# Spreading the modulation gradient's sums by pairs of bf16 products, and finishing the last section in two halves

## The chip, the cores and the metric

The kernel runs on one core of one Trainium2 chip. The metric is the device time of one execution in microseconds; several executions are timed and the median is given. Besides, one execution was recorded with the hardware profiler. PE is TensorE (PEld its weight loads), DVE VectorE, ACT ScalarE, POOL GpSimd, and SP SyncE, which here only issues DMAs. Each engine works through its own queue of instructions in order.

## The reference, cut to what matters

The reference is a block with two branches, forward, and its gradient with respect to all inputs for a given output gradient. x has 2048 rows of 576 columns.

```python
mod = (_silu(c) @ w_mod).reshape(c.shape[0], 6, 1, -1)
sa, ca, ga, sb, cb, gb = ...                      # six rows of 576
h = _layernorm(x) * (1 + ca) + sa
x = x + ga * _A_ref(h, A_w_r, A_w_i)              # 2-D FFT, filter, inverse FFT
h = _layernorm(x) * (1 + cb) + sb
x = x + gb * _B_ref(h, B_w_gate, B_w_up, B_w_down)  # (h Wg * h Wu) Wd
_out, _vjp = jax.vjp(_f, ...)
_grads = _vjp(grad_out)
```

The outputs are the block's result (out_0) and eight gradients. The change concerns the last two of them:

- out_8, the gradient of w_mod (576 x 3456). It falls into six sections of 576 columns, one for each of the six modulation rows. The gradient of a modulation row is a vector g of 576 numbers (a sum over all 2048 rows of x), and the section is the outer product of silu(c) and g.
- out_7, the gradient of c (576 numbers): for each row of w_mod the sum over all six sections of w_mod times g, and then times the derivative of silu.

For the sixth section, gb, the vector is the column sum of grad_out times the second branch's output.

## The kernel before, in words

Rows are dealt to 16 tiles of 128 partitions (row 16p + t lies in tile t). The stages follow one another: forward first branch, second branch's big products, the weight gradients, and then the tail, from line 731, in which the change lies. The tail has three transforms (t1, t2, t3: gradients back through the filter and the norms) and at last a loop over the 16 tiles (lines 1107 to 1149) that computes the second branch's output of each tile.

**The last loop.** Each tile t has two halves of 288 columns. For each half PE runs 36 matmuls (`u3p`, L1127) into a bank of PSUM, and ACT copies the bank to `ob` (L1128). DVE multiplies `ob` with the output gradient `got` to `pr` (L1134), then with the modulation row to `of` (L1136), and adds x1 (`x1t`) to `o0` (L1138), which a DMA on POOL's queue stores. `x1t` and `got` are loaded by POOL's queue for two tiles at a time, into one buffer each.

**Column sums.** A bank `csF` collects the sums of `pr` over all rows. `colsum` (L784) is a matmul with a table `pick` of ones that adds the first half of the columns on the bank's upper 64 rows and the second half on the lower 64. In the loop the sums of tile t - 2 are added after tile t's matmuls, and the last three tiles' after the loop's last matmuls. `add_zero` (L781) opens and closes the bank.

**Sections.** `section(j, halves, secp)` (L812) makes one sixth of out_8 and its share of out_7. Its vector first has to stand on all 128 partitions: `spread` (L803) multiplies it in float32 with a table (ones, `ones_f`, where the vector's parts are spread over rows, `of_rows`; a row selector, `sel`, where row 0 and row 64 hold the two halves, `of_sums`). Each of the two products leaves a bank with 288 columns; ACT copies the first to `dmb`, DVE the second (`evac`, L141 and L143). Then w_mod's section `wmj` is loaded by two DMAs on SP's queue (L817, L818); out_8's section `o8` is `dmb` scaled by silu(c), in five blocks of rows, shared by ACT (L832) and DVE or, in the last section, POOL (L834); two DMAs on SP's queue store it (L835, L836); and DVE multiplies `wmj` with `dmb` in five blocks, with a sum along the columns into `gsc` (L825). The buffers `dmb`, `wmj`, `o8` and `pr7` of the pool `secp` exist once.

Five sections are made within the loop, at tiles 9 to 13 (`late`, L1093, and L1129 to L1131). `tc.issue_after(mm.ins)` puts their PE instructions behind the tile's last matmul in PE's queue. The sixth, gb, follows the loop (L1150 to L1153): its sums are copied out of `csF` to `dgb`, spread, and finished with `last=True`, in which DVE's products come ahead of the scalings. Then (L1154 to L1168) `gsc` is summed, multiplied with the derivative (`gcf`), expanded to a 128 x 640 table (`gcd`) and turned into one row by two matmuls with ones, copied to `gcr` and stored as out_7.

**What sets the order.** The program lists instructions in the order of the Python text. A planner puts them into the engines' queues: it goes through a modelled time and gives each engine the instruction with the highest priority (the earliest in the program, where `tc.high_priority` does not change it) of those whose inputs it takes to be ready. It also adds the semaphores on which an instruction waits. On the chip a queue keeps this order whatever is late.

Of the kernel before, what the change touches and what calls it, by code (L numbers as in the profile page):

```python
# [19 lines left out]
NT = 16  # L20
S = 2048
D = 576
# [10 lines left out]
SPREAD = 40  # L33

# [50 lines left out]
def build(ctx, tc, A_x, A_w_r, A_w_i, B_w_gate, B_w_up, B_w_down, c_in, w_mod, grad_out,  # L85
# [39 lines left out]
    ones_f = glob.tile([128, 128], FP32, name="ones_f")  # L125
    nc.vector.memset(ones_f[:], 1.0)

# [603 lines left out]
    with ExitStack() as ts:  # L731
# [29 lines left out]
        sel = tl.tile([128, 2, 128], FP32, name="sel")  # L761
# [4 lines left out]
        gsc = tl.tile([128, 5, 6], FP32, name="gsc")  # L766
# [33 lines left out]
        def spread(lhs, src):  # L800

            pp = ps_fp.tile([128, 512], FP32, name="spp", tag="fp")
            nc.tensor.matmul(pp[:, 0:288], lhsT=lhs, rhs=src, start=True, stop=True)  # L803
            return pp[:, 0:288]

        def of_rows(d):
            return [lambda h=h: spread(ones_f[:], d[:, h * 288:(h + 1) * 288]) for h in range(2)]

        def of_sums(d):
            return [lambda h=h: spread(sel[:, h, :], d[:]) for h in range(2)]  # L810

        def section(j, halves, secp, last=False):  # L812
            dmb = secp.tile([128, D], FP32, name="dmb")
            for h in range(2):
                evac(dmb[:, h * 288:(h + 1) * 288], halves[h](), eng=("a" if h == 0 else "v"))
# [3 lines left out]
            o8 = secp.tile([128, 5, D], BF, name="o8")  # L819

            def products():
                for m in range(5):
                    r = RM[m]
                    pr7 = secp.tile([128, D], BF, name="pr7")
                    nc.vector.scalar_tensor_tensor(out=pr7[r, :], in0=wmj[r, m, :], scalar=1.0, in1=dmb[r, :], op0=MUL, op1=MUL, accum_out=gsc[r, m, j:j + 1])  # L825

            if last:
                products()
            for m in range(5):
                r = RM[m]  # L830
                if m % 2 == 0:
                    nc.scalar.activation(out=o8[r, m, :], in_=dmb[r, :], func=ACT.Copy, scale=sc_col[r, m:m + 1])  # L832
                else:
                    (nc.gpsimd if last else nc.vector).tensor_scalar(out=o8[r, m, :], in0=dmb[r, :], scalar1=sc_col[r, m:m + 1], scalar2=None, op0=MUL)  # L834
            nc.sync.dma_start(out_8[0:512, j * D:(j + 1) * D].rearrange("(m q) n -> q m n", q=128), o8[:, 0:4, :])  # L835
            nc.sync.dma_start(out_8[512:576, j * D:(j + 1) * D], o8[64:128, 4, :])  # L836
            if not last:
                products()
# [254 lines left out]
        late = {9: (MSB, of_sums(dsb)), 10: (MCB, of_rows(dcb)), 11: (MGA, of_rows(dga)), 12: (MSA, of_sums(dsa)), 13: (MCA, of_rows(dca))}  # L1093
# [12 lines left out]
        prs = {}  # L1106
        for tp_ in range(NT // 2):
# [13 lines left out]
            for ti in range(2):  # L1121
                t = 2 * tp_ + ti
                ob = o2p.tile([128, D], BF, name="ob3")
                for h in range(2):
                    p2 = ps_u3.tile([128, 512], FP32, name="u3p")
                    for fb in range(NFB):
                        mm = nc.tensor.matmul(p2[:, 0:288], lhsT=hls[fb // 9][:, fb % 9, ti * 128:(ti + 1) * 128], rhs=(wdA[:, fb] if fb < 15 else wdB[:, fb - 15])[:, h * 288:(h + 1) * 288], start=(fb == 0), stop=(fb == NFB - 1))  # L1127
                    nc.scalar.copy(ob[:, h * 288:(h + 1) * 288], p2[:, 0:288])  # L1128
# [3 lines left out]
                pr = prs[t] = o2p.tile([128, D], BF, name="pr3", bufs=3)  # L1132
                for h in range(2):
                    nc.vector.tensor_tensor(out=pr[:, h * 288:(h + 1) * 288], in0=ob[:, h * 288:(h + 1) * 288], in1=got[:, ti, h * 288:(h + 1) * 288], op=MUL)  # L1134
# [11 lines left out]
                for d_ in ([t - 2] if t < NT - 1 else [t - 2, t - 1, t]):  # L1146
# [80 lines left out]
```

## Time and profile before

| | us |
|---|---|
| median of three runs | 1588.66 (1585.04 to 1589.61) |
| profiled execution, its own time | 1585.66 |
| its span, first to last instruction | 1583.9 |
| granted TensorE clock, mean | 0.99 |
| PE busy, share of the span | 96% |
| DVE busy | 66% |
| ACT busy | 35% |
| POOL busy | 11% |
| last tile's last big matmul ends (u3p, L1127), from the span's start | 1569.7 |
| last instruction before the final store is issued (gcr, L1165) ends | 1580.9 |

Times within the execution count from the span's first instruction. A group of instructions is named by engine, line, output and inputs; "idle before" is the time for which the engine stood still ahead of it, and the arrow names what ended that. The chain of waits is followed back from the last instruction of the kernel.

### The profile page before, as it was taken

How to read it: one execution, taken by the hardware profiler on the slowest of the kernel's cores; microseconds unless marked ns; L12 is line 12 of the kernel's file. 1: busy time of each engine (PE TensorE's matmuls, PEld its weight loads, DVE VectorE, ACT ScalarE, POOL GpSimd, SP SyncE). 2: the span in 40 equal slices, each digit the busy share in tenths (PEclk: the TensorE clock that was granted, in tenths of full speed). 3: DMA queues.
4: the chain of work that ended last, by engine and by line, in shares of the span. 5: the costliest groups of instructions: out<-in, count | busy, mean ns of one | idle time of the engine just before them, and what ended most of it. 6: DMA issues, size and time to landing. Idle time of an engine off the chain costs nothing.

```text
span 1583.9 us, 29938 instructions
## 1 busy us (share of the span) xinstructions
PE 1526.4 (96%) x11300; PEld 1028.1 (65%) x11306; DVE 1043.3 (66%) x2626; ACT 559.4 (35%) x1120; POOL 172.3 (11%) x285
## 2 busy tenths in 40 slices
PE   6999999999999999999999999999999979799997
PEld 4665543566666666667666666766666666577775
DVE  6866663766666666666666666666666765678655
ACT  6667732322222222222222222222222356465022
POOL 0001221110010101001010100101000002000232
PEclk9999999999999999999999999999999999999999
DMA  9879997868685795877767786858976777547775
GB/s 323 268 197 235 289 261 211 172 133 158 123 177 114 159 153 118 168 132 155 141 148 136 143 163 122 173 116 144 139 141 137 193 207 200 212 144 214 278 228 156
DMA packets 485252, 280.33 MB, mean 177 GB/s; under 512 B 407634, under 2 KB 452435, under 8 KB 484211
## 3 DMA queue, kind: packets, MB, share of 16 engines
q1 hardware_dynamic: 459922, 185.50, 54.9%
q0 software_dynamic: 25184, 92.92, 19.7%
q8 instruction: 88, 1.44, 0.4%
q14 instruction: 58, 0.47, 0.1%
HBM read 108.48 MB, written 82.31 MB: 120 GB/s over the span
## 4 chain that ended last, share of the span: by engine, by line
PE 81%; DVE 6%; DMA 5%; issue 4%; ACT 3%; POOL 0%; SPq 0%; ACTq 0%; DVEq 0%; POOLq 0%
PE u57p L594 26%; PE u8p L676 18%; PE gup L647 16%; PE u4p L408 7%; PE u3p L1127 4%; PE gup L642 2%; DMA Xn<-xn_d 2%; DMA n2c<-n_d 2%; PE yp L186 1%; PE zp L908 1%; ACT u L1055 1%; PE zp L346 1%; DVE ln_st L151 1%; DMA xc<-in_A_x_dram 1%; DMA hh_sf<-hhT 1%
## 5 line engine op out<-in xcount | busy, mean ns | idle before, releaser
L681 DVE TENSOR_TENSOR acc<-acc,u8p 128x288 f32<-128x288 f32 x1088 | 489.2, 454 | 314.6 <-PE u8p L676 314.2
L676 PE MATMUL u8p<-wT,ggT 128*128 128x288 bf16 x1152 | 327.5, 286 | 1.7 <-DVE acc L681 1.7
L676 PE MATMUL u8p<-wT,guT 128*128 128x288 bf16 x1152 | 327.2, 286 | 0.0
L647 PE MATMUL gup<-h2T,wgu 128*128 128x512 bf16 x1152 | 294.9, 379 | 0.0
L597 ACT CAST so<-u57p 128x288 bf16<-128x288 f32 x216 | 86.0, 398 | 521.4 <-PE u57p L594 515.5
L594 PE MATMUL u57p<-gon,hh_sf 128*128 128x288 bf16 x1152 | 188.5, 286 | 0.5 <-DMA hh_sf<-hhT 0.5
L594 PE MATMUL u57p<-h2p,gg_sf 128*128 128x288 bf16 x1152 | 187.9, 286 | 0.0
L594 PE MATMUL u57p<-h2p,gu_sf 128*128 128x288 bf16 x1152 | 185.9, 286 | 0.0
L647 PEld LDWEIGHTS <-wgu 128*128 128x128 bf16 x1152 | 109.5, 98 | 98.8 <-issue 17.1
L676 PEld LDWEIGHTS <-ggT 128*128 128x128 bf16 x1152 | 112.6, 98 | 67.2 <-issue 14.0
L408 PE MATMUL u4p<-goT,wdT 128*128 128x512 bf16 x656 | 151.6, 380 | 0.6 <-DVE goT L380 0.5
L676 PEld LDWEIGHTS <-guT 128*128 128x128 bf16 x1152 | 112.7, 98 | 55.8 <-issue 2.2
L1127 PEld LDWEIGHTS <-hl 128*128 128x128 bf16 x1152 | 111.9, 99 | 32.9 <-issue 5.9
L594 PEld LDWEIGHTS <-hh_sf 128*128 128x128 bf16 x1152 | 112.7, 98 | 29.2 <-DMA hh_sf<-hhT 0.8
L594 PEld LDWEIGHTS <-gu_sf 128*128 128x128 bf16 x1152 | 112.5, 98 | 28.4
L594 PEld LDWEIGHTS <-gg_sf 128*128 128x128 bf16 x1152 | 112.5, 98 | 28.2
L649 ACT CAST gT<-gup 128x512 bf16<-128x512 f32 x144 | 84.3, 586 | 130.7 <-PE gup L647 130.7
L649 ACT CAST uT<-gup 128x512 bf16<-128x512 f32 x144 | 84.3, 585 | 73.5 <-PE gup L647 73.5
L408 PEld LDWEIGHTS <-wdT 128*128 128x128 bf16 x656 | 61.4, 98 | 73.1 <-issue 8.0
L1127 PE MATMUL u3p<-wdB,hl 128*128 128x288 bf16 x672 | 94.8, 290 | 5.3 <-DMA wdB<-in_B_w_down_dram 5.3
L660 POOL DMA_DIRECT2D hhT_d<-hhT x36 | 33.2, 921 | 504.4 <-DVE hhT L651 475.5
L141 ACT CAST ghh_st<-u4p 128x512 bf16<-128x512 f32 x88 | 51.2, 585 | 65.2 <-PE u4p L408 63.7
(357 smaller groups left out, 1701.7 us busy)
## 6 DMA issues: line engine op xcount, KB each, us to landing
ghhT_d<-ghh_st POOLq DMA_DIRECT2D x36, 512.0 KB, 4.4
ghh<-ghhT_d POOLq DMA_DIRECT2D x36, 512.0 KB, 7.3
hhT_d<-hhT POOLq DMA_DIRECT2D x36, 512.0 KB, 6.6
hl<-hhT_d SPq DMA_DIRECT2D x32, 576.0 KB, 7.2
out_dram<-woT SPq DMA_DIRECT2D x72, 128.0 KB, 2.0
wdn<-in_B_w_down_dram SPq DMA_DIRECT2D x18, 288.0 KB, 3.9
out_dram<-so SPq DMA_DIRECT2D x36, 144.0 KB, 2.6
wgu<-in_B_w_gate_dram SPq DMA_DIRECT2D x18, 256.0 KB, 3.4
```

The source lines that it names most:

```text
L141: nc.scalar.copy(dst, src)
L151: nc.vector.bn_stats(out=st[:, t, h, :], in_=xt[:, t, h * 288:(h + 1) * 288])
L408: nc.tensor.matmul(pt[:], lhsT=wdTs[k][:, j, m, :], rhs=goT[:, 4 * sb4:4 * sb4 + 4, m, :], start=(m == 0 and n == 5), stop=(m == n - 1))
L594: mm = nc.tensor.matmul(pw[0][:, 0:288], lhsT=sf[:, t, :], rhs=rhs_n[:, t, h * 288:(h + 1) * 288], start=(t == 0), stop=(t == NT - 1))
L597: nc.scalar.copy(so[:, h * 288:(h + 1) * 288], pw[0][:, 0:288])
L642: nc.tensor.matmul(pts[-1][:], lhsT=wgu[r, 8, jw * 128:(jw + 1) * 128], rhs=h2T[r, 4 * sb4:4 * sb4 + 4, 4, :], start=True, stop=False)
L647: nc.tensor.matmul(pts[k][:], lhsT=wgu[:, 4 * wi_ + m, jw * 128:(jw + 1) * 128], rhs=h2T[:, ts_, m, :], start=False, stop=(m == 3))
L649: nc.scalar.copy((gT, uT)[wi_][:, ts_, :], pts[k][:])
L660: nc.gpsimd.dma_start(hhT_d[:, :, fb, :].rearrange("tp f x -> f tp x"), hhT[:].rearrange("f (tp ti) p -> f tp (ti p)", ti=2))
L676: nc.tensor.matmul(pu[:, 0:288], lhsT=l_, rhs=r_, start=(k == 0), stop=(k == len(mms) - 1))
L681: nc.vector.tensor_tensor(out=dst, in0=dst, in1=pu[:, 0:288], op=ADD)
L1127: mm = nc.tensor.matmul(p2[:, 0:288], lhsT=hls[fb // 9][:, fb % 9, ti * 128:(ti + 1) * 128], rhs=(wdA[:, fb] if fb < 15 else wdB[:, fb - 1 ...
```

## The change

Four things change.

1. The vector is no longer spread by one float32 product. `two_parts` makes a bf16 copy (ACT) and the bf16 rest (DVE: the vector less the copy), and `spread` adds two bf16 products into the bank. `ones_f` goes, `sel` becomes bf16. The buffers of the two parts are of the pool `secp` and exist once for each of the two shapes (576 columns, `dr`, for cb, ga and ca; 288 columns, `ds`, for sb, sa and the sixth section's partial sum).
2. The sixth section's sums: `csF` collects tiles 0 to 10 only (`TURN`). At tile 12, after that tile's section, it is closed, and its two halves are spread by the row selector into two banks `csG`, on all 128 rows. The later tiles are added there by a product with ones (`ones_sum`), which leaves their sums on all rows too.
3. At the last tile, each half is finished by itself: DVE multiplies the bank of the big products with `got` directly, one matmul adds the sum to `csG`, and `last_half` scales and multiplies straight from that bank: five ACT instructions and five DVE products of 288 columns, and two stores on SP's queue. `wmj` of this section is loaded after the first half's matmuls. `dgb` and `dmb` are not used there, nor POOL. `gsc` has a seventh column for the second half.
4. The row of out_7 is made by five small matmuls with `gcf` itself as the stationary operand, one to a block of rows, in place of `gcd` and the two products; ACT copies 256 columns and DVE 320.

```diff
-    ones_f = glob.tile([128, 128], FP32, name="ones_f")
-    nc.vector.memset(ones_f[:], 1.0)
...
-        sel = tl.tile([128, 2, 128], FP32, name="sel")
+        sel = tl.tile([128, 2, 128], BF, name="sel")
...
-        gsc = tl.tile([128, 5, 6], FP32, name="gsc")
+        gsc = tl.tile([128, 5, 7], FP32, name="gsc")
...
+        def two_parts(pool, src, w, name):
+
+            hi = pool.tile([128, w], BF, name=name + "_hi")
+            lo = pool.tile([128, w], BF, name=name + "_lo")
+            nc.scalar.copy(hi[:], src)
+            nc.vector.tensor_tensor(out=lo[:], in0=src, in1=hi[:], op=SUB)
+            return hi, lo
+
+        def spread(out, lhs, parts, cols, stop=True):
+            for k, p_ in enumerate(parts):
+                nc.tensor.matmul(out, lhsT=lhs, rhs=p_[:, cols], start=(k == 0), stop=stop and k == 1)
+
+        def section_load(j, secp):
             wmj = secp.tile([128, 5, D], BF, name="wmj")
             nc.sync.dma_start(wmj[:, 0:4, :], w_mod[0:512, j * D:(j + 1) * D].rearrange("(m q) n -> q m n", q=128))
             nc.sync.dma_start(wmj[64:128, 4, :], w_mod[512:576, j * D:(j + 1) * D])
+            return wmj, secp.tile([128, 5, D], BF, name="o8")
+
+        def section_products(j, secp, wmj, sums, cols, slot):
+            for m in range(5):
+                r = RM[m]
+                pr7 = secp.tile([128, D], BF, name="pr7")
+                nc.vector.scalar_tensor_tensor(out=pr7[r, cols], in0=wmj[r, m, cols], scalar=1.0, in1=sums[r, :], op0=MUL, op1=MUL, accum_out=gsc[r, m, slot:slot + 1])
+
+        def section_store(j, o8, cols):
+            a0, a1 = j * D + cols.start, j * D + cols.stop
+            nc.sync.dma_start(out_8[0:512, a0:a1].rearrange("(m q) n -> q m n", q=128), o8[:, 0:4, cols])
+            nc.sync.dma_start(out_8[512:576, a0:a1], o8[64:128, 4, cols])
+
+        def section(j, d, secp):
+            rows = d.shape[1] == D
+            parts = two_parts(secp, d[:], d.shape[1], "dr" if rows else "ds")
+            dmb = secp.tile([128, D], FP32, name="dmb")
+            for h in range(2):
+                hs_ = slice(h * 288, (h + 1) * 288)
+                pp = ps_fp.tile([128, 512], FP32, name="spp", tag="fp")
+                spread(pp[:, 0:288], ones_b[:] if rows else sel[:, h, :], parts, hs_ if rows else slice(0, 288))
+                evac(dmb[:, hs_], pp[:, 0:288], eng=("a" if h == 0 else "v"))
+            wmj, o8 = section_load(j, secp)
...
+            section_store(j, o8, slice(0, D))
+            section_products(j, secp, wmj, dmb, slice(0, D), j)
+
+        def last_half(h, wmj, o8, secp, bank):
+            hs_ = slice(h * 288, (h + 1) * 288)
+            for m in range(5):
+                r = RM[m]
+                nc.scalar.activation(out=o8[r, m, hs_], in_=bank[r, 0:288], func=ACT.Copy, scale=sc_col[r, m:m + 1])
+            section_products(MGB, secp, wmj, bank[:, 0:288], hs_, 5 + h)
+            section_store(MGB, o8, hs_)
...
+        def ones_sum(t, h):
+            nc.tensor.matmul(csG[h][:, 0:288], lhsT=ones_b[:], rhs=prs[t][:, h * 288:(h + 1) * 288], start=False, stop=(t == NT - 1))
+
+        def sums(t):
+            for h in range(2):
+                if t > TURN:
+                    ones_sum(t, h)
+                else:
+                    colsum(csF, h, prs[t][:, h * 288:(h + 1) * 288])
+            if t == TURN:
+                add_zero(csF, first=False)
+                parts = two_parts(secp, csF[:, 0:288], 288, "ds")
+                for h, tag in enumerate(("csA", "csC")):
+                    csG.append(ps_cs.tile([128, 512], FP32, name="csG", tag=tag))
+                    spread(csG[h][:, 0:288], sel[:, h, :], parts, slice(0, 288), stop=False)
...
+                    if t == NT - 1:
+                        pr = pr_tile(t) if h == 0 else prs[t]
+                        nc.vector.tensor_tensor(out=pr[:, h * 288:(h + 1) * 288], in0=p2[:, 0:288], in1=got[:, ti, h * 288:(h + 1) * 288], op=MUL)
+                        if h == 0:
+                            last = section_load(MGB, secp)
+                            sums(t - 2)
+                            sums(t - 1)
+                        ones_sum(t, h)
+                        last_half(h, *last, secp, csG[h])
                     nc.scalar.copy(ob[:, h * 288:(h + 1) * 288], p2[:, 0:288])
...
-                for d_ in ([t - 2] if t < NT - 1 else [t - 2, t - 1, t]):
-                    for h in range(2):
-                        if d_ >= 0:
-                            colsum(csF, h, prs[d_][:, h * 288:(h + 1) * 288])
-        add_zero(csF, first=False)
-        dgb = tl.tile([128, 288], FP32, name="dgb")
-        nc.vector.tensor_copy(dgb[:], csF[:, 0:288])
-        section(MGB, of_sums(dgb), secp, last=True)
+                if 2 <= t < NT - 1:
+                    sums(t - 2)
...
-        gcd = secp.tile([128, 5, 128], BF, name="gcd")
-        nc.vector.tensor_tensor(out=gcd[:], in0=ident[:].unsqueeze(1).to_broadcast([128, 5, 128]), in1=gcf[:].unsqueeze(2).to_broadcast([128, 5, 128]), op=MUL)
         gcr = secp.tile([128, D], BF, name="gcr")
-        for m0, w in ((0, 4), (4, 1)):
+        for ms_, c0, w in (((0, 1), 0, 256), ((2, 3, 4), 256, 320)):
             pp = ps_fp.tile([128, 512], FP32, name="gcp", tag="fp")
-            nc.tensor.matmul(pp[:, 0:w * 128], lhsT=ones_b[:], rhs=gcd[:, m0:m0 + w, :].rearrange("p m n -> p (m n)"), start=True, stop=True)
+            for m in ms_:
+                r = RM[m]
+                nc.tensor.matmul(pp[0:1, m * 128 - c0:m * 128 - c0 + KD[m]], lhsT=gcf[r, m:m + 1], rhs=ident[r, 128 - KD[m]:128], start=True, stop=True)
...
```

47 lines of the change are left out of this document (14 added, 33 removed).

## The prediction

> **What bounds the kernel now.** I read the page's engine table first (PE is busy for 96% of the span), then the chain of waits in order of time, restricted to the last 85 us, then the timeline of each engine there, and last the tiles that the edits touch. The change acts only after 1450 us.
>
> The chain of waits, cut to the last stage; columns are start us, duration us, engine and line:
>
> ```profile
> 1510.48 0.97 PE spp L803 x4
> 1511.45 0.24 PE csF L784 x2
> 1511.69 8.82 PE u3p L1127 x72
> 1520.51 0.97 PE spp L803 x4
> ...
> 1560.90 8.83 PE u3p L1127 x72
> 1569.75 0.41 ACT ob L1128
> ...
> 1571.35 0.38 DVE dgb L1152
> 1571.73 0.04 issue
> 1571.78 1.25 PE spp L803 x4
> ```
>
> Until 1569.73 PE alone carries the chain: a tile of 72 matmuls takes 8.82 us (0.1225 each), and the spreading of a section stands between two tiles for 0.97 us. From there to the end, 14.2 us, the chain goes through single instructions. The timeline of the same stretch shows the costliest ones:
>
> ```profile
> 1573.60 2.23 ACT L832 ACTIVATE o<-dmb,sc_col 128x576 bf16<-128x576 f32 x3 [0.57 <-DVE dmb L143]
> 1573.60 0.76 DVE L825 SCALAR_TENSOR_TENSOR pr<-wmj,dmb 128x576 bf16<-128x576 bf16 x1
> 1573.68 4.29 POOL L834 TENSOR_SCALAR o<-dmb,sc_col 128x576 bf16<-128x576 f32 x2 [1.49 <-DVE dmb L143]
> 1574.40 1.18 DVE L825 SCALAR_TENSOR_TENSOR pr<-wmj,dmb 128x576 bf16<-128x576 bf16 x1
> ...
> 1578.86 0.83 DVE L1159 TENSOR_TENSOR gcd<-ident,gcf 128x640 bf16<-128x640 bf16 x1
> 1579.74 0.69 PE L1163 MATMUL gcp<-gcd,ones_b 128*128 128x512 bf16 x2 [6.72 <-DVE gcd L1159]
> 1580.36 0.57 ACT L1165 CAST gcr<-gcp 1x512 bf16<-1x512 f32 x1 [4.53 <-PE gcp L1163]
> 1580.96 0.32 SPq L1168 DMA_DIRECT2D out_dram<-gcr  x1
> ```
>
> DVE's five products go from 1573.60 to 1578.40, the two beside POOL's work taking 1.18 instead of 0.76. From the last copy's end (1580.93) to the span's end (1583.9) it is 2.95 us: the small store. Third, DVE's timeline at tile 10, where DVE is late:
>
> ```profile
> 1523.43 0.45 DVE L143 COPY dmb<-spp 128x288 f32<-128x288 f32 x1
> 1528.67 0.46 DVE L1138 TENSOR_TENSOR o<-of,x1t 128x576 bf16<-128x576 bf16 x1 [4.79 <-DMA x1t<-x_d]
> 1529.04 0.94 DVE L834 TENSOR_SCALAR o<-dmb,sc_col 128x576 bf16<-128x576 f32 x2
> 1530.25 0.76 DVE L825 SCALAR_TENSOR_TENSOR pr<-wmj,dmb 128x576 bf16<-128x576 bf16 x1 [0.26 <-DMA wmj<-in_w_mod_dram]
> ```
>
> DVE's products of tile 10's section start when PE is already at the end of tile 11 (1530.38). Those of the sections end at 1522.5, 1534.2, 1544.4, 1554.1 and 1562.3, paced by DMA (an x1t load, then wmj loads of 4 to 8 us), not by PE. PE does not notice, because nothing it needs from DVE is younger than two tiles.
>
> **The change part by part.**
>
> *Spreading in bf16.* Per section four float32 instructions (0.97 us) go and four bf16 matmuls of 288 columns (4 x 0.1225 = 0.49) come: 0.48 less on PE, five sections, **-2.4 us**.
>
> *What comes ahead of the last big matmul.* The sum of tiles 0 to 10 is spread early (four matmuls, 0.49, and a zero matmul of 512 columns, 0.22), the four column sums of tiles 13 and 14 move between the halves of tile 15 (0.49), and one sum of tile 15 with them (0.12): **+1.3 us**. The last big matmul ends 1.1 us earlier, at T = 1568.6.
>
> *High and low parts.* Each section now needs an ACT copy (128x576 from float32: 0.67 by the copy of the accumulator; 288: 0.40) and a DVE subtraction (float32 operands: 256 columns 0.42, 512 columns 0.68, so 576 about 0.75 and 288 about 0.45). ACT has 3.4 us of work per 10 us tile and DVE 5 to 8, so the busy time is hidden. The first two pairs can fall into the third transform's last steps at 1451 to 1457, where PE already waits 0.3 us at a time for ACT: 0 to 1.3 us, taken as 0, since the waiting ACT shows there is room. The order is the question: PE now waits for the subtraction, which stands in DVE's queue, in front of tensor products that wait for DMAs or behind them. For tile 11 the parts can be made only after tile 10's spreading has read the shared buffer (1520.9). In DVE's queue the subtraction then comes either before the instruction that waits for x1t (done at 1524: no wait), after the two scalings (1530.7), or after the products (1534.9). PE wants it at about 1529.4, with two savings behind it. So the wait is 0, 1.3 or 5.5 us. For the partial sum at tile 12 DVE can do it at about 1546 (products to 1544.4, then four instructions); PE arrives between 1541 and, if the planner put it late, after that: 0 to 5 us, and 7.5 if it stands behind the next products (1554.1). Those waits do not add fully, as DVE's clock is set by DMA: together 0 to 8 us. I take 0, by the row that shows the long DVE gap (4.79 us idle right where the subtraction is ready), and keep 8 for the range.
>
> *Tile 15, first half.* It ends 5.0 us before T (36 x 0.1225 plus the 0.6 moved in), 1563.6. DVE is free at 1563.8; product from the bank 0.45 (the accumulating addition of 288 columns out of a bank takes 0.454), sum matmul 0.38 with its hand-overs, five ACT scalings of 288 columns at 0.40 after the copy of the tile: 1564.7 to 1566.7. The wmj load starts at 1562.4, when the previous products free the buffer, and lands 3.7 to 5.0 us after its second part's issue at 1562.83: 1566.5 to 1567.8. Five products of 288 columns at 0.50 (0.80 from start to start at 576, less 288 columns at 1.02 ns): done 1569.3 to 1570.3. They precede the second half's product in the program, so that one starts 0.7 to 1.7 after T; I take **+1.2**. Queued behind it: the final sum and all that follows.
>
> *Tile 15, second half, and the finish.* Product 0.45; sum matmul 0.38; then five ACT scalings (2.0) and five DVE products (2.5) that read the same bank. In the trace of before every bank is read by one engine; no row shows two readers at once. If they run side by side the scalings cost nothing, one after the other 2.0 us. I take 2.0, since the nearest rows have a single reader. [...] Then the reduction 0.22, the product with the derivative 0.21, five small matmuls instead of the 0.83 expansion and two big ones (0.6 with latency, from the 0.28 of one matmul and four more behind it), the wider of the two copies (320 columns, 0.5), and the store 2.95. Sum: 0.45 + 0.38 + 2.0 + 2.55 + 0.22 + 0.21 + 0.6 + 0.5 + 2.95 = 9.9 us. The tile's own copy and output (0.40, 0.45, 0.45) fill DVE's wait for ACT; if that cover goes, 0.9 more. Both `dmb` copies, the float32 spreading (1.25), dgb, POOL's 4.29 and the slowed products go.
>
> *Queues.* SP issues four stores of the last section in place of two (0.85 us more), the first pair during the second half, the second pair at about T + 4.3, well ahead of the small store. POOL loses its two scalings. The removed ones table and the smaller selector stand in idle time: nothing.
>
> Sum: end at 1568.6 + 1.2 + 9.9 = 1579.7 against 1583.9, **-4.2 us**; on the profiled execution's own time 1581.5 (1585.66). That execution lies 3.0 us under the median of the runs shown; the four known executions average 1587.2, 1.6 above it, and I add these 1.6: **1583.1**, 0.35% under the median of 1588.66. I call 0.3% (4.8 us) about what a measurement of this kernel can tell from no change.
>
> **The rivals.**
>
> Side by side (0.19): ACT and DVE read the bank together. For: their data are ready at the same moment. Against: no row with two readers. -2.0: 1581.1.
>
> A short wait of PE (0.25): one subtraction stands after the scalings, or the partial sum's comes 2 to 4 us late. For: DVE's section work runs a tile behind PE. Against: DVE's idle 4.79 us. +3: 1586.1.
>
> A long wait (0.14), the one that ends slower: tile 11's subtraction stands behind tile 10's products in DVE's queue, because the planner believes wmj landed. PE stops 5.5 us at 1529, and again 2.5 at the partial sum: 8.0 in all, 1591.1. It decides from 5.6 us of waiting on. For: products are older in the program, and DVE did each section's five in one piece. Against: at 1523.9 wmj was 6 us from landing.
>
> The spreading saves nothing (0.05): if a pair of bf16 matmuls with its loads took the 0.97 again, 1585.5. Against: the colsum pairs take 0.24 on the chain.
>
> My own forecast has 0.37, with 1581 to 1585.5 as its own range.
>
> **How the numbers follow.** Faster by over 0.3% means under 1583.9: 0.6 of the forecast (0.22), nearly all of side by side (0.19), 0.06 of the others: 0.47. Slower by over 0.3%, above 1593.4: 0.04 of the long wait and 0.06 for an order changed elsewhere: 0.10. Same: 0.43. The range goes from side by side with the second half's 1.2 gone (1578.5) to the long wait (1591).
>
> **What would show it.** Right: in the chain, spreading of 0.49 between tiles and no PE wait for a subtraction; the last big matmul at 1568.6; scalings, then products, after it; 11 us to the end. Wrong: idle PE before a spreading, released by DVE; a last big matmul after 1571; scalings and products overlapping.

## The result, and the profile after

The changed kernel takes 1598.9 us (median of 7 executions, 1592.62 to 1609.42), against 1588.66 us for the kernel before (7 executions, 1585.04 to 1591.26). The ratio is 1.0078, with a 95% interval of 1.0057 to 1.01 (the two medians divided give 1.0064): the change makes the kernel slower by 0.8%, where I had forecast 1583.1 us, 0.35% faster. The profiled execution after took 1602.71 us, with a span of 1600.9 us.

The view to read first is again the chain of waits, here of the kernel after, from tile 10 on (start us, duration us, engine and line):

```profile
1530.46 8.38 DMA wmj<-in_w_mod_dram
...
1540.67 0.67 DVE dr_lo L803
...
1543.86 5.88 DMA wmj<-in_w_mod_dram
...
1554.78 6.78 DMA wmj<-in_w_mod_dram
...
1563.39 0.38 DVE ds_lo L803
1563.78 0.04 issue
1563.82 0.64 PE csG L808 x2
1564.46 6.97 PE u3p L1162 x47
1571.42 0.49 PE spp L808 x4
1571.91 0.24 PE csG L1127 x2
1572.16 8.82 PE u3p L1162 x72
```

In the kernel before, PE carried this stretch alone. Now, up to 1563.8, the chain runs through three loads of `wmj`, DVE's products that wait for them, and the subtraction that makes a low part; PE takes over only after that. The spreading of a section itself costs 0.49 us, as forecast. What PE waited for in the last stage (us in total, number of waits, longest):

```profile
PE csG L808 <- DVE ds_lo L803: 3.6, 1, 3.6
PE csG L808 <- ACT ds_hi L802: 3.2, 1, 3.2
PE spp L808 <- DVE dr_lo L803: 3.1, 1, 3.1
...
PE csG L1127 <- DVE pr L1165: 1.0, 1, 1.0
```

The first three are new: the low part of tile 11's section (3.1 us), and the high and the low part of the partial sum (3.2 and 3.6 us), 9.9 us together. DVE's and PE's timelines show the place of the last (start, duration, engine, line, output and inputs, and in brackets the idle time before it and what ended that):

```profile
1561.58 0.76 DVE L820 SCALAR_TENSOR_TENSOR pr<-wmj,dmb 128x576 bf16<-128x576 bf16 x1 [4.89 <-DMA wmj<-in_w_mod_dram]
...
1562.63 0.75 DVE L820 SCALAR_TENSOR_TENSOR pr<-wmj,dmb 128x576 bf16<-128x576 bf16 x1
...
1563.31 0.45 DVE L803 TENSOR_TENSOR ds_lo<-csF,ds_hi 128x288 bf16<-128x288 f32 x1
1563.68 0.75 DVE L820 SCALAR_TENSOR_TENSOR pr<-wmj,dmb 128x576 bf16<-128x576 bf16 x1
```
```profile
1563.82 0.64 PE L808 MATMUL csG<-ds_lo,sel 128*128 128x288 bf16 x2 [3.55 <-DVE ds_lo L803]
1564.25 2.76 PE L1162 MATMUL u3p<-wdB,hl 128*128 128x288 bf16 x11
```

ACT had made `ds_hi` by 1555.6, but the subtraction stands in DVE's queue behind the first two products of tile 12's section (and an addition between them), and the first product waits for its load. DVE does nothing for 4.89 us, with the subtraction ready, because the instruction at the head of its queue is not.

The wait of 3.2 us for the high part comes the same way by one more step, as ACT's timeline shows:

```profile
1554.87 0.40 ACT L139 COPY dmb<-spp 128x288 f32<-128x288 f32 x1 [3.44 <-DVE pr L820]
1555.16 0.41 ACT L802 CAST ds_hi<-csF 128x288 bf16<-128x288 f32 x1
```

The copy that makes `ds_hi` stands in ACT's queue behind the copy of a section to `dmb`. That one needs the only `dmb` buffer, which DVE's products of the section before free at 1554.75, after they had waited 4.00 us for their own load.

The next view is PE's clock: the same profile cut into stretches (length, then busy time of PE, PEld, DVE, ACT and POOL, the granted TensorE clock, the DMA share, GB/s):

```profile
1542.00:1550.80 8.80, 8.80 (x74) 7.04 (x72) 4.70 (x15) 3.58 (x6) 1.56 (x3) 1.00 0.76 215
1555.90:1560.20 4.30, 4.30 (x22) 2.78 (x21) 0.79 (x2) 1.90 (x3) 0.00 (x0) 0.60 0.93 236
1563.80:1567.20 3.40, 3.38 (x16) 2.22 (x16) 2.17 (x6) 0.15 (x1) 2.60 (x4) 0.56 0.63 196
1567.20:1571.20 4.00, 4.00 (x35) 3.19 (x33) 0.31 (x1) 0.25 (x1) 0.00 (x0) 1.00 0.86 181
```

After the two waits for the partial sum the granted clock is 0.60 and 0.56, and a matmul takes about 0.25 us (2.76 us for 11) instead of 0.1225. Against full speed that costs some 1.6 and 1.2 us, 2.8 together, by my estimate from these rows.

The end is shorter, as forecast. From the last big matmul (1590.76) to the span's end it is 10.1 us, against 14.2 before:

```profile
1592.20 2.19 ACT L850 ACTIVATE o<-csG,sc_col 128x288 bf16<-128x288 f32 x5
```
```profile
1594.42 0.45 DVE L820 SCALAR_TENSOR_TENSOR pr<-wmj,csG 128x288 bf16<-128x288 bf16 x1 [1.27 <-ACT o L850]
```

DVE's first product out of the bank waits until ACT's fifth scaling out of the same bank is done.

The account, from the start of tile 9's spreading, which all kernels have at the same place of the program, to the end: 73.6 us before, 82.0 after, so 8.4 more. Of that the stretch to the last big matmul has 59.4 and 71.9 (+12.5: waits 9.9, slow clock 2.8, the rest savings, moved work and small gaps), and the finish 14.2 and 10.1 (-4.1). The other 8.6 us of difference between the two spans (1600.9 less 1583.9 is 17.0) lie ahead of that point. Experiments 1 and 2 look at them first.

### The profile page after: what moved, and what is told of

Read it like the earlier page. It is cut to its first block, busy times and chain, and to the rows that moved or that the text cites. A ratio compares the mean times of both kernels' runs of the same rounds, so it can differ in the third digit from the quotient of the medians.

```text
span 1600.9 us, 29965 instructions
## 1 busy us (share of the span) xinstructions
PE 1528.2 (95%) x11303; PEld 1027.2 (64%) x11309; DVE 1043.6 (65%) x2638; ACT 563.2 (35%) x1132; POOL 167.9 (10%) x283
## 4 chain that ended last, share of the span: by engine, by line
PE 76%; DMA 8%; DVE 8%; issue 4%; ACT 3%; POOL 0%; SPq 0%; ACTq 0%; DVEq 0%; POOLq 0%
PE u57p L592 25%; PE u8p L674 17%; PE gup L645 15%; PE u4p L406 7%; PE gup L640 2%; DMA xc<-in_A_x_dram 2%; DMA Xn<-xn_d 2%; DMA n2c<-n_d 2%; PE u3p L1162 2%; DMA wmj<-in_w_mod_dram 1%; PE zp L922 1%; DVE ln_st L149 1%; DVE pr L820 1%; PE zp L344 1%; PE yp L184 1%
```

## The experiments

My theory from these rows: PE waits for parts that DVE makes late, or ACT behind DVE, because DVE's queue stands before a transfer. All ratios are against the kernel before, run beside each.

In this table the stretch is counted in the profile from the start of tile 9's spreading to the end of the last big matmul, and the finish from there to the span's end.

| kernel | stretch, us | finish, us | ratio (95% interval) |
|---|---|---|---|
| before | 59.4 | 14.2 | 1 |
| changed | 71.9 | 10.1 | 1.0078 (1.0057 to 1.01) |
| 1 ones kept | 72.8 | 10.2 | 1.006 (1.0036 to 1.0084) |
| 2 before, addresses shifted | 59.5 | 14.2 | 1.0001 (0.9977 to 1.0025) |
| 3 no waits for low parts | 66.1 | 9.7 | 1.0014 (0.9991 to 1.0038) |
| 4 float32 sections | 68.4 | 10.2 | 1.0054 (1.0033 to 1.0074) |
| 5 pairs in the loop alone | 59.0 | 14.9 | 1.0024 (1.0003 to 1.0044) |
| 6 partial sum spread late | 64.7 | 10.2 | 1.0006 (0.9988 to 1.0024) |
| 7 as 3, two load buffers | 59.6 | 10.2 | 0.9977 (0.9954 to 0.9999) |
| 8 as 7, sum copied out of the bank | 60.7 | 9.3 | 0.9982 (0.9958 to 1.0006) |
| 9 before, two load buffers | 62.0 | 14.2 | 1.001 (0.9989 to 1.0031) |
| 10 changed, two load buffers | 67.1 | 10.2 | 1.0042 (1.0021 to 1.0063) |
| 11 as 8, two x1t buffers | 60.1 | 9.2 | 0.9973 (0.9953 to 0.9993) |
| 12 changed, three buffers doubled | 59.9 | 10.1 | 0.9964 (0.9943 to 0.9985) |
| 13 as 11, two o8 buffers | 58.4 | 9.3 | 0.995 (0.9933 to 0.9967) |
| 14 before, three buffers doubled | 59.4 | 14.2 | 0.999 (0.9971 to 1.0009) |

### 1 and 2: does it matter that buffers lie elsewhere?

The profile after was 8.6 us late before the sections began. The removed table of ones shifts earlier buffers by 512 bytes, so this is the first rival to test. Experiment 1 is the changed kernel with the table put back:

```diff
+    ones_f = glob.tile([128, 128], FP32, name="ones_f")
+    nc.vector.memset(ones_f[:], 1.0)
```

> The changed kernel with the removed float32 table of ones put back where it stood (allocated and filled, used by nothing). All queues keep the changed kernel's order except for this one DVE instruction; every buffer gets back the address that it had before the change (512 bytes per partition further). In the profiles the changed kernel is 9.5 us late at 284 us already, long before the edited code. Theory address shift: this loss goes, the forward stage's last u4p matmul again near 273 us, median about 1589. Rival, that this loss is only a difference between executions: median about 1599 as for the changed kernel, the last u4p matmul anywhere from 273 to 284 us. Both expect PE's waits for the low parts (3.1, 3.2 and 3.6 us) to stay.

Measured: 1597.25 us, ratio 1.006. Experiment 2 is the kernel before with the table moved into the tail's pool, so that its earlier buffers lie as in the changed kernel:

```diff
-    ones_f = glob.tile([128, 128], FP32, name="ones_f")
-    nc.vector.memset(ones_f[:], 1.0)
...
+        ones_f = tl.tile([128, 128], FP32, name="ones_f")
+        nc.gpsimd.memset(ones_f[:], 1.0)
```

> The kernel before with its float32 table of ones allocated in the tail's pool and filled by POOL there, so that it computes the same, and all buffers of the earlier stages lie 512 bytes lower, as in the changed kernel. Theory address shift: slower by about 9 us, median 1597. Rival, difference between executions: same as before, 1588.7 within 3.

Measured: 1588.99 us, ratio 1.0001. The addresses do nothing that this measurement shows; its interval is about 4 us wide on either side. The early lateness differs from execution to execution: the profiled one of experiment 1 reached tile 9's spreading at 1510.33, that of the kernel before at 1510.31, that of after at 1518.87, and over all profiles of this study the point lies between 1505.5 and 1518.9. Most of that spread is there long before the edited code: the forward stage's last group of `u4p` matmuls starts at 270.13 in the kernel before, at 280.14 in the one after, and at 278.51 in experiment 4, which has the table of ones in its old place. What is compared from here on is therefore the stretch from tile 9's spreading.

### 3: take the waits for low parts away

The rows' pair gets two buffers, so that tile 11's parts need not wait for tile 10's spreading, and the partial sum is spread behind tile 14's matmuls:

```diff
-            lo = pool.tile([128, w], BF, name=name + "_lo")
+            lo = pool.tile([128, w], BF, name=name + "_lo", bufs=2 if name == "dr" else 1)
...
-                    spread(csG[h][:, 0:288], sel[:, h, :], parts, slice(0, 288), stop=False)
...
+                if t == NT - 2:
+                    with tc.issue_after(mm.ins):
+                        spread_sums()
```

(the high part's buffer likewise; the bank is then opened by the first sum of ones).

> As e1_ones_kept, but PE no longer waits for the low parts: the pair for 576 columns has two buffers, so that tile 11's parts are made before tile 10's section, and the partial sum's spreading is put behind tile 14's matmuls (the later tiles' sums start the banks). Theory waits: against e1 the three waits (9.9 us) and the half-speed matmuls behind them (2.8 us) go, 12.5 us faster than e1, about 5 us faster than before. Rival, the section work on DVE, now longer by the subtractions, sets the end whatever PE does: at most 4 us faster than e1, and DVE's last section ends as late as in e1.

Measured: 1589.79 us, ratio 1.0014. Most of the loss is gone, so the waits carried it, but the gain of the shorter finish does not show. PE's waits in this kernel say why:

```profile
PE csG L1130 <- DVE pr L1190: 3.4, 1, 3.4
PE csG L1130 <- DVE pr L1173: 1.5, 2, 0.9
...
PE u3p L1170 <- ACT ob L1180: 1.2, 1, 1.2
```

The sums of tiles 13 and 14 now stand between the halves of tile 15, and there PE meets the same late DVE: tile 14's product is made at 1570.22, behind the products of tile 13's section, which waited 5.13 us for `wmj`. The big matmuls behind these waits run at half speed again (14 in 3.35 us). The waits removed at tiles 11 and 12 came back here as 3.4 us at tile 15, as DVE was still late.

### 4 and 5: the parts one by one

Experiment 4 has the partial sum and the new finish, but the five sections are spread in float32 as before (with a float32 selector beside the bf16 one):

```diff
-                spread(pp[:, 0:288], ones_b[:] if rows else sel[:, h, :], parts, hs_ if rows else slice(0, 288))
+                nc.tensor.matmul(pp[:, 0:288], lhsT=ones_f[:] if rows else sel_f[:, h, :], rhs=d[:, hs_ if rows else slice(0, 288)], start=True, stop=True)
```

> As e1_ones_kept, but the five sections within the loop are spread by float32 products as before; only the partial sum and the last section are as in the change. Theory waits: the 3.1 us at tile 11 go and 2.4 us of PE come back, and the partial sum's waits (6.8 us and the slow clock) stay: within 2 us of e1. Rival, the pairs' parts on ACT and DVE are what makes the partial sum late: the waits at the partial sum shrink below 3 us and the kernel is 4 us or more faster than e1.

Measured: 1597.4 us, ratio 1.0054; PE waited 4.1 us for `ds_hi` and 1.5 for `ds_lo`. Experiment 5 is the other part, the kernel before with pairs in the five sections of the loop and the old finish:

```diff
-        late = {9: (MSB, of_sums(dsb)), 10: (MCB, of_rows(dcb)), 11: (MGA, of_rows(dga)), 12: (MSA, of_sums(dsa)), 13: (MCA, of_rows(dca))}
+        late = {9: (MSB, dsb), 10: (MCB, dcb), 11: (MGA, dga), 12: (MSA, dsa), 13: (MCA, dca)}
...
+            if not last:
+                halves = pair(halves, secp)
```

(`pair` makes the parts and two bf16 products for each half.)

> The kernel before, with only the five sections of the loop (tiles 9 to 13) spread by pairs of bf16 products; the sum of the last section is spread as in before, in float32 after the loop. My theory (the gain of 0.48 us per spreading is given back where PE waits for a low part whose subtraction stands in VectorE's queue behind products that wait for their load) expects one wait of about 3 us before tile 11's spreading and none of more than 1 us elsewhere, against 2.4 us gained: +0.5 us, 1588 to 1591, ratio 0.999 to 1.002. First rival, the pairs alone carry the slowdown (each section makes PE wait): +7 us or more, ratio over 1.004. Second rival, without the partial sum the planner finds a place for every subtraction: -2.4 us, ratio about 0.9985.

Measured: 1591.53 us, ratio 1.0024, somewhat above what I had expected. The wait at tile 11 is there (1.8 us), the stretch is 0.4 us shorter than before and the finish 0.7 longer; that is 0.3 us in the profile, just under the interval's lower end (0.5 us), so most of the difference that the ratio gives (3.8 us) does not show in it; the two medians of this experiment divided give 1.0013, or 2.0 us. The two parts, 0.54% and 0.24%, add to the 0.78% of the whole, but each has an interval of about 0.2% on either side, so that the exact sum is luck. The larger part is the partial sum with the new finish.

### 6: the partial sum alone put later

Experiment 1 with only the second edit of experiment 3; tile 11's pair keeps its one buffer.

```diff
-                    spread(csG[h][:, 0:288], sel[:, h, :], parts, slice(0, 288), stop=False)
...
+                if t == NT - 2:
+                    with tc.issue_after(mm.ins):
+                        spread_sums()
```

> The changed kernel with the float32 table of ones kept, and the pair of the partial sum spread only behind tile 14's matmuls instead of before tile 13's; tile 11's pair keeps its single buffer. My theory expects the wait of about 3 us before tile 11's spreading to stay and the waits before tile 13's first matmul (5.0 and 1.6 us with the ones kept) to go, with the half-speed stretch behind them (2.8 us): 1591 to 1594, ratio 1.002 to 1.004, between the kernel with both waits (1.006) and that with neither (1.0014). Rival, what costs is that the sums of tiles 13 and 14 and their products stand between the halves of tile 15: then the time stays at 1597, ratio 1.006.

Measured: 1589.01 us, ratio 1.0006, better than I had expected and no worse than experiment 3, though the wait at tile 11 is there (3.4 us, with a half-speed stretch behind it). Time that PE loses at tile 11 is time that DVE gains on it: at tile 15 PE did not wait for tile 14's product in this kernel, where it had waited 3.4 us in experiment 3. So the waits do not simply add up: here the lateness that PE waits out at tile 11 is not met again at tile 15. In the changed kernel PE meets it twice, at tile 11 and at the partial sum.

### 7 and 8: let the section's load start earlier

Experiment 7 adds a second buffer for `wmj` to experiment 3, and gives up two buffers of the activations for it:

```diff
-            wmj = secp.tile([128, 5, D], BF, name="wmj")
+            wmj = secp.tile([128, 5, D], BF, name="wmj", bufs=2)
...
-        hlp = pool("hlp", 7, "right", stack=rA)
+        hlp = pool("hlp", 5, "right", stack=rA)
```

> The kernel without waits for low parts (two buffers for the rows' pairs, the partial sum spread behind tile 14), and in it two buffers instead of one for a section's tile of weights (wmj), so that a section's load starts while the products of the section before still read the other; to make room, two buffers of the up-projection's activations move away. My theory says that VectorE is late at tile 15 because each section's products wait 5 to 8 us for a load that the single buffer holds back: then the waits of 3.4 and 1.5 us of PE for VectorE's products of tiles 13 and 14 go, tile 15's halves come without a stop, and the time is 1582 to 1585, ratio 0.996 to 0.998. Rival, the loads wait because the DMA engines are busy, not for the buffer: ratio 1.000 to 1.002, as with one buffer, with products that still wait 4 us or more for wmj.

Measured: 1586.54 us, ratio 0.9977. No product waits for `wmj` any more, the wait for tile 14's product has gone, and the stretch is 59.6 us. Experiment 8 copies each half of the last sum out of its bank first:

```diff
+            dmb = secp.tile([128, D], FP32, name="dmb")
+            nc.vector.tensor_copy(dmb[:, hs_], bank[:, 0:288])
...
-                nc.scalar.activation(out=o8[r, m, hs_], in_=bank[r, 0:288], func=ACT.Copy, scale=sc_col[r, m:m + 1])
-            section_products(MGB, secp, wmj, bank[:, 0:288], hs_, 5 + h)
+                nc.scalar.activation(out=o8[r, m, hs_], in_=dmb[r, hs_], func=ACT.Copy, scale=sc_col[r, m:m + 1])
+            section_products(MGB, secp, wmj, dmb[:, hs_], hs_, 5 + h)
```

> As the kernel with two load buffers, and in it each half of the last section's sum is copied by VectorE out of the bank into a tile of the on-chip buffer first (288 columns, about 0.45 us), and ScalarE's five scalings and VectorE's five products read that tile. My theory says that in the changed kernel the five products start only after the fifth scaling because both read one bank: from the copy on they should overlap, which saves 2.0 us of scalings and costs 0.45 of copy, 1.5 us less from the last matmul to the end than the kernel with two load buffers: about 8.5 us instead of 10, ratio 0.001 lower. Rival, the order comes from the instructions' order in the program or from the semaphores, not from the bank: the products still start after the scalings, and the tail is 0.45 us longer.

Measured: 1586.7 us, ratio 0.9982, not to be told from experiment 7 by time. The finish fell from 10.2 to 9.3 us, less than the 1.5 expected, and in the timeline the scalings and the products overlap:

```profile
1567.64 2.37 ACT L855 ACTIVATE o<-dmb,sc_col 128x288 bf16<-128x288 f32 x5 [0.50 <-DVE dmb L852]
1567.88 0.45 DVE L823 SCALAR_TENSOR_TENSOR pr<-wmj,dmb 128x288 bf16<-128x288 bf16 x1
```

With the sum read from the on-chip buffer the first product starts 0.24 us after the first scaling, with the sum read from the bank it started after the fifth. So the order comes with the shared bank. The program itself keeps it: in the kernel after, the row of DVE's first product names ACT's scaling as what ended its wait. The rest of the expected gain went to DVE's two instructions for the tile's output (0.45 us each), which had filled its wait for ACT and now stand between or ahead of the products.

### 9 and 10: the second load buffer by itself, and in the changed kernel as it is

Experiment 9 puts the edit of experiment 7 into the kernel before, experiment 10 into experiment 1.

> The kernel before with nothing of the change in it, but with two buffers for a section's tile of weights (and two buffers of the up-projection's activations moved away to make room). A control: in before PE waits for nothing that VectorE makes in the sections, and the last section's load lands before its sum is ready, so by my theory a second buffer gains nothing there: ratio 0.999 to 1.001. Rival: the second buffer is a gain by itself and not what the change lacked; then the time falls by 3 us or more as in the changed kernels that have it, ratio about 0.998.

Measured: 1588.11 us, ratio 1.001: nothing gained, as expected. (In its profile PE waited 2.4 us for a copy of ACT's, which accounts for its longer stretch.)

> The changed kernel (with the float32 table of ones kept), in which only the section's tile of weights has two buffers instead of one; the partial sum is spread before tile 13's matmuls as in the changed kernel, and the pair of rows has one buffer. My theory says that the subtractions are late because the products in front of them in VectorE's queue wait for a load that the single buffer holds back: the waits of PE of 5.0 and 2.9 us for low parts fall below 1.5 us each, the half-speed stretches behind them go too, and the time falls from 1.006 to between 0.997 and 1.000 of before. Rival: the waits come from where the partial sum and the pairs are placed, whatever the load does; then at least one wait of 3 us stays and the ratio is 1.003 or more.

Measured: 1593.26 us, ratio 1.0042, so my theory in this form was wrong: waits of 3.9 us for `ds_lo` and 2.6 for `dr_lo` stayed. DVE's timeline of this kernel shows what it waited for instead:

```profile
1535.13 0.46 DVE L1186 TENSOR_TENSOR o<-of,x1t 128x576 bf16<-128x576 bf16 x1 [3.32 <-DMA x1t<-x_d]
1536.18 0.75 DVE L806 TENSOR_TENSOR dr_lo<-dga,dr_hi 128x576 bf16<-128x576 f32 x1
...
1553.52 0.95 DVE L845 TENSOR_SCALAR o<-dmb,sc_col 128x576 bf16<-128x576 f32 x2 [3.55 <-DMA out_dram<-o]
1556.11 0.45 DVE L806 TENSOR_TENSOR ds_lo<-csF,ds_hi 128x288 bf16<-128x288 f32 x1
```

No load of `wmj` is left in front of the subtractions, but the load of `x1t` is, and the store of `o8`, which holds the only buffer that the scalings can write to. Either the theory holds for any transfer ahead of the subtraction, or the place itself is too early; experiment 12 tells these apart.

### 11 to 14: the other two buffers

Experiment 11 is experiment 8 with two buffers of `x1t`:

```diff
-            x1t = o2p.tile([128, 2, D], BF, name="x1t3", bufs=1)
+            x1t = o2p.tile([128, 2, D], BF, name="x1t3", bufs=2)
```

> The kernel with two load buffers and the last section's sum copied out of the bank, and in it also two buffers instead of one for the tile of the residual input (x1t), with one more buffer of the up-projection's activations moved away. There PE still waited 1.5 and 0.5 us between the halves of tile 15 and 0.5 us at tile 14, behind a VectorE that had waited 7.4 us for the load of x1t. My theory expects those waits to fall under 0.5 us together: 2 us less, ratio 0.996 to 0.997. Rival: that load is late because the DMA engines are busy; then nothing changes, ratio 0.998.

Measured: 1583.65 us, ratio 0.9973. The waits at tile 15 fell from 2.1 to 0.5 us, but the wait for ACT's copy of a tile grew from 0.5 to 1.5; against experiment 8 the difference is within the intervals. Experiment 12 is experiment 10 with that edit and two buffers of `o8`, one buffer more of the activations given up for each:

```diff
-            return wmj, secp.tile([128, 5, D], BF, name="o8")
+            return wmj, secp.tile([128, 5, D], BF, name="o8", bufs=2)
```

> The changed kernel with two load buffers of a section's weights, and in it two buffers as well for the section's scaled rows (o8, which VectorE's scalings wait for until its stores are out) and for the residual input (x1t); two more buffers of the up-projection's activations are moved away. The instructions of VectorE and of ScalarE stand in the same order as with the weights' load doubled alone, so only what they wait for differs. My theory, mended: a subtraction is late by whatever transfer the instructions ahead of it wait for, and with the load of the weights doubled it was the store of o8 (3.6 us) and the load of x1t (3.3 us). Then the waits of PE of 3.9 and 2.6 us fall below 1 us each and the time to 0.996 to 0.999 of before. Rival, the place: by the time that PE wants them the parts cannot be made, because VectorE and ScalarE have too much work ahead of them; then waits of 2 us or more stay and the ratio is 1.002 or more.

Measured: 1585.08 us, ratio 0.9964. The place of the spreading and the order of DVE's and ACT's instructions are those of experiment 10, and the waits are gone:

```profile
PE csG L1130 <- DVE pr L1168: 1.0, 1, 1.0
PE csG L811 <- ACT ds_hi L805: 0.9, 1, 0.9
PE csG L811 <- DVE ds_lo L806: 0.2, 1, 0.2
```

The subtractions for tile 11 and for the partial sum have no waiting instruction close ahead of them in this profile, and the stretch is 59.9 us with 1.1 us of waits in it, where experiment 13 has 58.4 without: by my estimate from these, at most some 0.4 us is left for matmuls at a slow clock. That decides for the transfers and against the place; how much each of the two buffers added here is worth, no run separates. Experiment 13 puts the `o8` edit into experiment 11:

> The kernel with two load buffers, two of x1t, the partial sum spread late and the last sum copied out of the bank, and in it two buffers for o8. There VectorE's scalings still waited 5.4 us three times for the store of o8, but PE waited for VectorE only 0.5 us and for ScalarE's copy of a tile 1.5 us. My theory: the 1.5 us go at most, 1 to 2 us less, ratio 0.9955 to 0.997. Rival: PE has nothing left to wait for in this stage and the time stays at 0.9973.

Measured: 1582.6 us, ratio 0.995 (0.9933 to 0.9967). This has the lowest ratio of the study, though its interval overlaps those of experiments 11 and 12: faster than the kernel before by 0.5% and than the changed one by 1.3% (0.995 over 1.0078). Its stretch is 58.4 us, and PE's only wait for DVE before the end, 0.5 us, comes just behind it. Experiment 14 gives the three doubled buffers to the kernel before (and moves its small buffer `dgb` into the sections' pool):

> The kernel before with nothing of the change, but with the three kinds of buffers doubled that the changed kernel got (a section's weights, its scaled rows, the residual input) and the same number of the up-projection's activations moved away; VectorE's and ScalarE's instructions stand in the order of before. A control: PE waits for nothing of VectorE's in the sections of before, so the buffers should gain nothing there: ratio 0.998 to 1.002. Rival: the buffers are a gain by themselves, and the changed kernel that has them is faster for that reason; then 0.997 or less.

Measured: 1587.19 us, ratio 0.999, with an interval that holds 1. The buffers by themselves gain nothing that can be measured; with the change they turn 1.006 into 0.9964. What the change needed is that DVE be on time.

## Why the prediction was wrong, and where it was right

**Spreading in bf16, -2.4 us: right.** The chain has 0.49 us for a pair of halves where it had 0.97, five times.

**What comes ahead of the last big matmul, +1.3 us, so 1.1 us less to that point: right in size.** Experiment 13, in which PE waits for nothing of DVE's in the stretch, has 58.4 us instead of 59.4, 1.0 less.

**High and low parts, "I take 0": wrong, and this is the step that failed.** The waits were 3.1 us at tile 11 and 6.7 at the partial sum, 9.9 together, over the upper end of "0 to 8". The matmuls at half speed behind them cost 2.8 us more. Over the stage I had forecast 69.4 us (73.6 less 4.2); 82.0 came, 12.6 more, about what the waits and the slow matmuls come to (12.7). My step listed the right places: in front of the waiting instruction, behind the scalings, behind the products. It then chose the first, by the row with DVE's 4.79 us of idle time. That reading was mistaken. The idle time belonged to an instruction at the head of DVE's queue that waited for `x1t`; what stands behind such an instruction waits too, as the subtraction did in the kernel after, ready while DVE stood still for 4.89 us, and the row shows that DVE is held there, not that it is free. The subtraction went behind the second of five products, a place that I had not listed, because in the profile before the five stood together. And I had counted ACT's copy as hidden work and only the subtraction as something to wait for: 3.2 of the 9.9 us were waited for the copy, behind the one `dmb` buffer.

The rival "a long wait" was what happened, with 8.0 us of waiting foreseen against 9.9. I had put 5.5 at tile 11 and 2.5 at the partial sum; it was the other way round, 3.1 and 6.7. Its time of 1591.1 was still 7.8 short of the median. Part of that is 1.9 us more waiting and 2.8 us of half-speed matmuls after the waits, which no term of mine had. I had counted against that rival that at 1523.9 `wmj` was 6 us from landing. The load was late indeed, and the subtraction was put behind products that need it all the same: the lateness spoke for the wait.

**Tile 15, first half, +1.2: a little high.** The second half's product started 0.5 us after the last big matmul, and PE waited 1.04 us for it, the product's own 0.46 included.

**The finish: 1.2 + 9.9 = 11.1 forecast, 10.1 measured.** The choice of 2.0 us for scalings and products that read the same bank one after the other, which no row of before showed, was right: 2.2 us of scalings, then the products (DVE's first starts at 1594.42, after 2.19 us of ACT's scalings from 1592.20), and an overlap as soon as both read the copy in experiment 8. What the chip would do without that order, no run here shows. "Side by side" is refuted for this program.

**"The spreading saves nothing" is refuted** by the 0.49 us.

**The rest of the sum was sound.** Experiment 12 has the change as it stands (with the float32 ones kept) and only the cause of the waits removed, and its ratio times the median before, 0.9964 x 1588.66, is 1582.9 us, against my 1583.1. The ratio's interval is over 3 us wide on either side, so that a match this close is luck; the stage says it better, 70.0 us against the 69.4 forecast. A part of the gain, up to 0.3%, could be the buffers' own by the interval of experiment 14. What failed is one term, in which I let one idle stretch decide over a chance of 0.14.

**What stays open.** In the profile the stage accounts for 8.4 us of the change, and the medians differ by 10.2. By the interval of the ratio, 9.1 to 15.9 us, some of the loss may lie ahead of tile 9's spreading. Experiment 4, 5.0 us in the stage against a ratio worth 8.6, shows the same. Executions differ there by up to 13 us in the profiles, and in the profile after, the first pair of parts is made only at 1461.05, while the lateness was there at 280. From the third transform's last matmuls (`yp`, starting at 1452.55 before and 1461.05 after) to tile 9's spreading it is 57.8 us in both. So the changed instructions did not cause the lateness of that profile; whether the changed kernel is late there more often than the one before, single profiles cannot tell. No run moved the subtraction ahead of the products while the buffers stayed single, which would test the queue's order directly.

## What to carry to other kernels

DVE's idle time here was free only for instructions ahead of the waiting one in its queue: in the kernel after it stood still for 4.89 us with the subtraction ready behind. Before a new dependency is put through an engine that is idle "while waiting for DMA", look at which instruction holds its queue and at how many buffers that transfer has. If a fast engine is to need a slow one's result soon, first take the single-buffered transfers out of the slow one's path: here that gained nothing alone (0.999) and was worth 1% with the change. Removing the waits at tiles 11 and 12 (9.9 us in the changed kernel) while DVE stayed late left one of 3.4 us at tile 15, the next place where DVE was needed (experiment 3), so remove what makes the engine late.

## What the runs showed of the hardware

My forecast had no term for a fall of PE's clock after a wait. Experiment 10 has both sides in one profile, in the columns of the windows above: the first row follows the wait of 2.61 us at tile 11, the second the wait of 3.9 us at the partial sum.

```profile
1537.00:1541.00 4.00, 4.00 (x20) 2.61 (x20) 3.90 (x12) 1.43 (x3) 2.16 (x4) 0.57 0.86 287
```
```profile
1556.60:1560.00 3.40, 3.38 (x28) 2.71 (x28) 2.47 (x7) 0.40 (x1) 2.61 (x4) 1.00 0.97 299
```

After the shorter wait the granted clock is 0.57 over 4.0 us (15 matmuls take 3.65 us instead of 2.00), after the longer one it stays at 1.00. In the kernel after, tile 11's wait of 3.13 us left the clock at 1.00, and in experiment 1 the same wait of 2.90 us brought it to 0.61. In experiment 6, after a wait of 3.36 us, the half speed lasted longer:

```profile
1533.90:1540.00 6.10, 6.10 (x28) 3.85 (x28) 4.28 (x12) 3.19 (x5) 2.17 (x4) 0.54 0.61 155
```

There 28 matmuls took 6.1 us at a mean granted clock of 0.54, where 28 of 0.1225 would take 3.4. So in these runs a wait of 2.6 us cost another 1.7 us (experiment 10), and waits of 3.13 us (the kernel after) and 3.9 us (experiment 10) cost nothing more: the length of the wait alone does not decide it. What does, no run here shows.
